# Spectral layers: one stored difference of sequence blocks fewer, formed anew in the second sweep

## The chip, the cores and the metric

The kernel runs on one core of one Trainium2 chip. The metric is the device time of one execution in microseconds (us); the kernel before is given as the median of its runs. The engines of the core are named as in the profile: PE (matmuls) and PEld (its weight loads), DVE (elementwise), ACT (copies, casts, activations), POOL (elementwise) and SP, which here issues the transfers between the chip's memory and the core's on-chip buffers in one queue, in order.

## The reference

Four layers follow each other on x of shape 2048 x 640 (sequence x features), each with a layer norm ahead of it and a residual add behind it: an attention over a dilated window, a spectral layer, and both again.

```python
def _B_ref(x, dft_seq_re, dft_seq_im, dft_hid_re, dft_hid_im):
    a = jnp.einsum("bsd,ed->bse", x, dft_hid_re)
    b = jnp.einsum("bsd,ed->bse", x, dft_hid_im)
    # Real((Cr + i*Ci) @ (a + i*b)) = Cr@a - Ci@b
    y = jnp.einsum("ts,bse->bte", dft_seq_re, a) - jnp.einsum("ts,bse->bte", dft_seq_im, b)
    return y

x = A_x
x = x + _A_ref(_layernorm(x, axis=-1), A_wqkv, A_wo)
x = x + _B_ref(_layernorm(x, axis=-1), B_dft_seq_re, B_dft_seq_im, B_dft_hid_re, B_dft_hid_im)
x = x + _A_ref(_layernorm(x, axis=-1), A_wqkv, A_wo)
x = x + _B_ref(_layernorm(x, axis=-1), B_dft_seq_re, B_dft_seq_im, B_dft_hid_re, B_dft_hid_im)
```

`_A_ref` is the window attention (32 heads of 20, 8 keys at distance 2); the change does not touch it. `_B_ref` is the spectral layer. All data are float32.

## The kernel before

The layers are numbered 0 to 3; 1 and 3 are the spectral ones (`LayerB`, with `self.li` 1 or 3). Such a layer multiplies first by the sequence matrices and then by the hidden ones. Each float32 operand is split into a rounded part (`hi`, cast by ACT, L1137) and its residual (`lo`, subtracted by DVE, L1138); a product then takes three passes of matmuls: hi times hi, hi times lo, lo times hi (`PASSES`, `product`, matmuls on L1148).

The sequence matrices arrive as `cs`, eight tiles of 256 outputs (real and imaginary part side by side) by 16 blocks of 128 rows. A raw block is 128 x 512 float32, 256 KB. Tiles 0 and 1 are worked with plain products (L1004). Tiles 2 to 7 are worked in three pairs (`pair(p)`, tiles t1 = 2p+2 and t2 = 2p+3) by a scheme of seven products in place of eight, as Strassen's in Winograd's form. For step i of eight, the four blocks are b11 = (t1, i), b21 = (t1, i+8), b12 = (t2, i) and b22 = (t2, i+8), and the scheme needs beside b11, b21, b22 these differences:

- x1 = b12 - b11 (the stored "t1")
- x3 = b22 - b12 (the stored "t3")
- x2 = b22 - x1
- x4 = b21 - x2

A pair has two sweeps over the eight steps. The first sweep takes the products with the plain blocks: aux (banks q), t (banks r) and m (banks w), and, for the features that the scheme leaves over, xt and pq (f1, f2) with all four blocks. The second sweep takes the products with x2 (banks q, "aux" in the profile), x3 (r, "t"), x4 (w, "m") and x1 (y, "xt" and "pq"). After it ACT and DVE combine the banks (L1301 to L1313) and store the result to `zb`.

In layer 1 only (`sums`), the first sweep also forms x1 and x3 on DVE (L1225, in place, in the buffers of b11 and b12) and stores both to the chip's memory, to `tb` (L1227). The second sweep, in both layers, loads x1 and x3 from `tb` (L1221) and b22 and b21 from `cs` (L1126), and forms x2 and x4 on DVE (L1225), each in place: x2 overwrites b22, x4 overwrites b21.

Raw blocks go through nine buffers in rotation (five "win", two "xa", two halves of "e2", L1204); split blocks (views) through eight in layer 1, ten in layer 3 (L1205). A buffer is loaded again when its readers are done, a store out of it included. PE's order is the program's order. The order of DVE, ACT and SP is made at build time by a scheduler with modelled times, so that work of later steps and pairs stands among that of earlier ones. In layer 1 the first sweeps also prepare the hidden weights on ACT and DVE (`b_prep`, L1161 to L1197); in the last pair's second sweep the operands of the hidden stage are prepared (`hid_load`, `prep`, L1328 and L1357), whose matmuls are on L1393.

## Time and profile before

| | |
|---|---|
| runs of the kernel before | 1699.35, 1698.45, 1706.01 us; median 1699.35 us |
| span of the profiled execution | 1700.9 us, 1.55 us above the median of the runs; no other time of that execution is listed |
| granted PE clock over the span | 1.000 |
| memory read and written | 319.75 MB and 119.67 MB, 258 GB/s over the span |
| layer 1, from the first product of the first pair to the hidden stage | 439.7 to 735.2 us |
| layer 3, the same | 1280.4 to 1574.2 us |

The page gives busy time and share of the span by engine; below it, chains and waits name what an engine stood waiting for. "DVE zo L1138" reads as the instruction of line 1138 on DVE that writes a buffer named zo. A row of the stretches gives the start and end, the length, then each engine's busy time with the number of its instructions. In the timeline a row starts with its start and its duration; idle time ahead of it stands in square brackets with what ended it. Instructions of one engine overlap a little in it: on DVE a following instruction of 0.68 us can start 0.60 us after the one ahead.

### The profile page before, as it was taken

The page shows a single profiled execution, that of the slowest core. Times are in us where ns is not written, and L with a number is a line of the kernel's source. Part 1 is how long each engine was busy: PE and PEld are TensorE (multiplying, and loading weights), DVE is VectorE, ACT ScalarE, POOL GpSimd, SP SyncE. Part 2 cuts the span into 40 slices and gives each one's busy share as a digit, 9 for nine tenths or more (in the row PEclk, how much of TensorE's full clock was granted, in tenths as well). Part 3 has the DMA queues.
Part 4 walks back from the last instruction along what each step waited for, and adds up shares of the span by engine and source line. Part 5 has one row for each costly group of instructions (what it writes and reads, how often), then busy time and mean ns, then how long its engine had stood idle before and what let it go on. Part 6 is the DMA issues. An engine that isn't in the chain of part 4 may idle for free.

```text
span 1700.9 us, 25512 instructions
## 1 busy us (share of the span) xinstructions
PE 1679.7 (99%) x8558; PEld 1464.6 (86%) x8558; DVE 1339.2 (79%) x2034; ACT 794.0 (47%) x1617; POOL 625.8 (37%) x588
## 2 busy tenths in 40 slices
PE   9999999989999999999999999999999999999999
PEld 7888988868888887899988889988888888888999
DVE  6999999978588786788639999999784656657784
ACT  5664644544354443536554335444444544444231
POOL 4899999950000000000028988999400000000000
PEclk9999999999999999999999999999999999999999
DMA  8996668857899989986377866788666776787942
GB/s 295 315 322 227 221 227 307 271 206 265 287 370 322 370 270 354 351 331 225 122 226 239 270 217 204 246 284 295 212 234 208 225 228 215 242 282 270 362 164 93
DMA packets 263139, 441.13 MB, mean 259 GB/s; under 512 B 21824, under 2 KB 126016, under 8 KB 260704
## 3 DMA queue, kind: packets, MB, share of 16 engines
q1 hardware_dynamic: 259808, 437.55, 75.7%
q10 hardware_dynamic: 3200, 1.97, 0.4%
q8 instruction: 67, 1.10, 0.3%
q14 instruction: 64, 0.52, 0.1%
HBM read 319.75 MB, written 119.67 MB: 258 GB/s over the span
## 4 chain that ended last, share of the span: by engine, by line
PE 76%; DVE 10%; POOL 6%; DMA 4%; issue 2%; ACT 0%; SPq 0%; DVEq 0%; POOLq 0%; ACTq 0%
PE m L381 19%; PE t L1148 7%; PE aux L1148 7%; PE m L1148 7%; PE pq L1148 5%; PE xt L1148 5%; PE m L1393 4%; PE aux L1393 4%; PE m L1004 3%; PE t L1004 3%; DVE pr L450 2%; PE aux L531 2%; DVE pr L490 2%; POOL pr L509 2%; PE xt L1393 2%
## 5 line engine op out<-in xcount | busy, mean ns | idle before, releaser
L381 PE MATMUL m<-r,s 128*128 128x480 f32 x1920 | 434.5, 381 | 0.6 <-ACT stg L388 0.4
L381 PEld LDWEIGHTS m<-r,s 128*128 128x128 f32 x1920 | 355.4, 188 | 53.5 <-ACT stg L388 0.8
L193 POOL TENSOR_TENSOR stats<-stats,mhalf 128x1 f32<-128x1 f32 (+1 forms) x40 | 29.2, 730 | 512.2 <-ACT stats L189 503.8
L509 POOL TENSOR_TENSOR pr<-pr 128x640 f32<-128x640 f32 x126 | 207.8, 1650 | 23.1 <-DVE pr L490 21.7
L450 DVE TENSOR_TENSOR pr<-pq,win 128x1280 f32<-128x1280 f32 x128 | 189.9, 1484 | 13.8 <-DMA win<-kvb 7.8
L490 DVE TENSOR_TENSOR pr<-pq,win 128x1280 f32<-128x1280 f32 x128 | 190.3, 1487 | 3.7 <-POOL zo L511 1.2
L453 POOL TENSOR_TENSOR pr<-pr 128x640 f32<-128x640 f32 x115 | 164.9, 1434 | 11.2 <-DVE pr L450 11.2
L460 DVE TENSOR_REDUCE lg<-pr 128x64 f32<-128x640 f32 (+1 forms) x128 | 112.7, 881 | 8.0 <-POOL pr L453 7.9
L510 POOL TENSOR_TENSOR pr<-pr 128x320 f32<-128x320 f32 x126 | 112.0, 889 | 9.9
L388 ACT COPY stg<-m 128x480 f32<-128x480 f32 x128 | 71.0, 555 | 92.9 <-PE m L381 69.1
L1004 PE MATMUL m<-s,r 128*128 128x512 f32 x366 | 111.2, 392 | 1.6 <-DMA s<-c0b 1.3
L1004 PE MATMUL t<-s,r 128*128 128x512 f32 x366 | 110.3, 390 | 0.0
L531 PE MATMUL aux<-r2a,ot 128*128 128x320 f32 x540 | 84.7, 310 | 0.7 <-ACT s L369 0.7
L531 PEld LDWEIGHTS aux<-r2a,ot 128*128 128x128 f32 x540 | 81.1, 188 | 2.8 <-ACT s L369 1.2
L1004 PEld LDWEIGHTS m<-s,r 128*128 128x128 f32 x366 | 67.6, 188 | 16.1 <-DMA s<-c0b 1.9
L1004 PEld LDWEIGHTS t<-s,r 128*128 128x128 f32 x366 | 68.7, 188 | 14.5
L1137 ACT CAST zo<-win 128x512 fp32r<-128x512 f32 x76 | 47.2, 621 | 65.4 <-PE xt L1148 30.0
L423 ACT COPY pq<-qs 128x320 f32<-128x320 f32 x64 | 27.5, 430 | 106.0 <-DVE pr L490 73.4
L1138 DVE TENSOR_TENSOR zo<-win,zo 128x512 fp32r<-128x512 f32 x76 | 52.1, 688 | 23.7 <-ACT zo L1137 23.3
L511 POOL TENSOR_TENSOR zo<-pr 128x160 f32<-128x160 f32 x126 | 67.1, 532 | 9.9
L1004 PE MATMUL xt<-s,r 128*128 128x512 f32 x183 | 68.6, 389 | 0.0
L468 ACT ACTIVATE lg<-lg 128x128 f32<-128x128 f32 x64 | 20.3, 317 | 74.6 <-DVE lg L479 74.4
(531 smaller groups left out, 3650.2 us busy)
## 6 DMA issues: line engine op xcount, KB each, us to landing
win<-cs_in SPq DMA_DIRECT2D x192, 256.0 KB, 3.8
win<-kvb SPq DMA_DIRECT2D x96, 440.0 KB, 5.3
win<-kvb SPq DMA_DIRECT2D x64, 360.0 KB, 5.0
kvb<-stg SPq DMA_DIRECT2D x60, 320.0 KB, 4.9
xa<-cs_in SPq DMA_DIRECT2D x66, 256.0 KB, 3.6
e<-cs_in SPq DMA_DIRECT2D x64, 256.0 KB, 3.9
r<-zb SPq DMA_DIRECT2D x12, 1280.0 KB, 5.9
win<-tb SPq DMA_DIRECT2D x56, 256.0 KB, 4.4
```

The source lines that it names most:

```text
L381: nc.tensor.matmul(mt[g][:, : 3 * F], st[:, a, k], wq[q][:, b, k], start=n == 0, stop=n == 14)
L388: nc.scalar.copy(sgs[q][:, :, j % 2], mt.pop(g)[:, : 3 * F].rearrange("p (a f) -> p a f", f=FE))
L450: nc.vector.tensor_tensor(pr, q, wview(u, jp, 0, [[1, FE]]), op=ALU.mult)
L453: nc.gpsimd.tensor_tensor(pv[:, :, 0:10], pv[:, :, 0:10], pv[:, :, 10:20], op=ALU.add)
L460: nc.vector.tensor_reduce(lgs[u][:, :, 2 * jp : 2 * jp + 2].rearrange("p h j w -> p (j w) h"), prq.pop((u, jp)), axis=AX.X, op=ALU.add,)
L490: nc.vector.tensor_tensor(pr.rearrange("p j w (h d) -> p j w h d", d=DH), lgs[u][:, :, 2 * jp : 2 * jp + 2].rearrange("p h j w -> p j w h" ...
L509: g.tensor_tensor(pr[:, :, 0:4], pr[:, :, 0:4], pr[:, :, 4:8], op=ALU.add)
L510: g.tensor_tensor(pr[:, :, 0:2], pr[:, :, 0:2], pr[:, :, 2:4], op=ALU.add)
L531: nc.tensor.matmul(m[:, :320], oT[(c, j)][:, a, k], wo_s["w"][:, b, k, e * 320 : (e + 1) * 320], start=(i, k) == (0, 0), stop=(i, k) == (2 ...
L1004: self.last = nc.tensor.matmul(self.z[t][k], self.xn[c][:, a, j, k * P : (k + 1) * P], self.ct[s][:, b], start=s == 0 and i == 0, stop=s = ...
L1148: nc.tensor.matmul(bank, w(a, kb), hl[b], start=start and (a, b) == (0, 0), stop=stop and (a, b) == (1, 0), skip_group_check=True,)
L1393: nc.tensor.matmul(bank[:, :320], s[:, a, k], w[:, b], start=start and (k, a, b) == (0, 0, 0), stop=stop and (k, a, b) == (KD - 1, 1, 0), ...
```

## The change

The difference x3 = b22 - b12 is no longer formed and stored in the first sweep of layer 1. In the second sweep, in both layers, b12 is loaded from `cs` in the place of x3 from `tb`, and DVE forms x3 in b12's buffer, ahead of x2 because x2 overwrites b22. `tb` keeps one difference per step, x1.

```diff
-    tb = [dr.tile([P, NP, 2, 512], F32, name=f"tb_{p}") for p in range(NPAIR)]
+    tb = [dr.tile([P, NP, 512], F32, name=f"tb_{p}") for p in range(NPAIR)]
...
-            def t_sum(n, i, o, a, b):
+            def t_sum(o, a, b):
                 v.tensor_tensor(o, a, b, op=ALU.subtract)
-                if n in names:
-                    nc.sync.dma_start(t_slot(n, i), o)
                 return o
...
                     if sums:
-                        t_sum("t1", i, b11, b12, b11)
-                        t_sum("t3", i, b12, b22, b12)
+                        nc.sync.dma_start(t_slot(i), t_sum(b11, b12, b11))
...
-                    x1, b22, x3, b21 = t_raw("t1", i), raw(t2, NP + i), t_raw("t3", i), raw(t1, NP + i)
+                    x1, b22, b12, b21 = t_raw(i), raw(t2, NP + i), raw(t2, i), raw(t1, NP + i)
                     s1, s2, s3 = (self.x_slot(m, i, XTAGS) if last and (m, i) in self.xlate else self.x_kept(m, i) for m in (1, 2, 3))
-                    x2 = t_sum("t2", i, b22, b22, x1)
+                    x3 = t_sum(b12, b22, b12)
+                    x2 = t_sum(b22, b22, x1)
                     self.product(q, s2, split(x2), False, i == NP - 1)
                     self.product(r, s3, split(x3), *ends)
-                    x4 = t_sum("t4", i, b21, b21, x2)
+                    x4 = t_sum(b21, b21, x2)
                     self.product(w, self.x_plain(*k2(i), 256), split(x4), *ends)
                     self.product(y, s1, split(x1), *ends)
```

In all, 24 subtractions and 24 stores of 256 KB leave layer 1's first sweeps; 48 subtractions enter the second sweeps; 48 loads of 256 KB read `cs` and no longer `tb`. The scheduler's order changes with it on DVE, ACT and SP, in the pairs and at the start of layer 1's hidden stage; PE's and POOL's orders are the same row for row. In the new file the subtraction is on L1223, the store on L1264, the load from `tb` on L1219, and the lines behind the pair stand four lower.

SP at the start of the third pair of layer 1, first sweep. Before (win_6517 is the buffer of a b12, xa_6567 that of a b11):

```order
L1227 DMA tb_146<-win_6517 128x512
L1126 DMA win_6633<-cs_in 128x512
L1027 DMA zb_5_133<-s_955_6042 512x1x128
L1126 DMA win_6688<-cs_in 128x512
L1227 DMA tb_146<-xa_6567 128x512
L1227 DMA tb_146<-win_6572 128x512
L1126 DMA e_724_4650<-cs_in 128x512
L1126 DMA win_6692<-cs_in 128x512
L1109 DMA zo_1067_6695<-xc_4_124 128x512
```

After:

```order
L1126 DMA win_6668<-cs_in 128x512
L1126 DMA e_724_4650<-cs_in 128x512
L1264 DMA tb_146<-xa_6547 128x512
L1126 DMA win_6725<-cs_in 128x512
L1126 DMA win_6729<-cs_in 128x512
L1264 DMA tb_146<-xa_6606 128x512
L1126 DMA e_724_4650<-cs_in 128x512
L1126 DMA win_6781<-cs_in 128x512
```

The stores out of the win buffers of b12 are gone; the loads into those buffers, which stood behind them, have no store to wait for.

DVE at the turn from the first to the second pair of layer 1: the adds that empty the banks (L1303 to L1311 before, L1299 to L1307 after), among splits and sums of the next pair. Before:

```order
L149 TENSOR_TENSOR pr_934_5916<-pr_906_5730,pr_934_5916 128x2x320
L1225 TENSOR_TENSOR win_5565<-e_724_4650,win_5565 128x512
L1303 TENSOR_TENSOR s_809_5153<-t_811_5163,s_808_5152 128x512
L1303 TENSOR_TENSOR s_809_5153<-t_812_5164,s_808_5152 128x512
L1138 TENSOR_TENSOR zo_895_5630<-xa_5621,zo_895_5630 128x512
L1138 TENSOR_TENSOR e_896_5639<-win_5623,e_896_5639 128x512
```

After (L147 and L149 are pieces of `b_prep`):

```order
L1305 TENSOR_TENSOR s_809_5137<-xt_5151,s_809_5137 128x512
L1307 TENSOR_TENSOR s_807_5135<-xt_5151,s_807_5135 128x512
L1138 TENSOR_TENSOR stg_5638<-e_724_4650,stg_5638 128x512
L147 SCALAR_TENSOR_TENSOR pr_953_6014<-pr_943_5954,pr_953_6014 128x2x32
L1138 TENSOR_TENSOR ot_5656<-win_5616,ot_5656 128x512
L1305 TENSOR_TENSOR s_809_5137<-pq_5152,s_809_5137 128x512
L1307 TENSOR_TENSOR s_807_5135<-pq_5152,s_807_5135 128x512
```

The next pair's x3 sum (L1225 on win_5565) no longer stands ahead of the adds, nor does the piece of L149; the piece of L147 now stands ahead of the last two.

DVE in the last step of the third pair's second sweep, layer 1. Before (L1225 on win_7310 is x2, on win_7314 x4; L1138 out of xa_7312, win_7310, win_7308 are the residuals of x3, x2, x1; L1366 prepares the hidden stage):

```order
L1225 TENSOR_TENSOR win_7310<-win_7310,win_7308 128x512
L1366 TENSOR_TENSOR r_2_1154_7205<-r_0_1153_7202,r_2_1154_7205 128x640 x2
L1138 TENSOR_TENSOR e_1177_7327<-xa_7312,e_1177_7327 128x512
L1138 TENSOR_TENSOR zo_1176_7318<-win_7310,zo_1176_7318 128x512
L1225 TENSOR_TENSOR win_7314<-win_7314,win_7310 128x512
L1138 TENSOR_TENSOR ot_7346<-win_7308,ot_7346 128x512
```

After (x3 on xa_7287, x2 on win_7285, x4 on win_7289):

```order
L1362 TENSOR_TENSOR r_2_1154_7178<-r_0_1153_7175,r_2_1154_7178 128x640 x2
L1223 TENSOR_TENSOR xa_7287<-win_7285,xa_7287 128x512
L1223 TENSOR_TENSOR win_7285<-win_7285,win_7283 128x512
L1138 TENSOR_TENSOR e_1177_7303<-xa_7287,e_1177_7303 128x512
L1223 TENSOR_TENSOR win_7289<-win_7289,win_7285 128x512
L1138 TENSOR_TENSOR ot_7322<-win_7283,ot_7322 128x512
L1138 TENSOR_TENSOR zo_1176_7294<-win_7285,zo_1176_7294 128x512
```

The residual of x2 (zo) now has x3, x4 and the residual of x1 (ot) ahead of it that stood behind it, or nowhere, before.

## The prediction

> **What bounds the kernel now.** I read the page's busy shares first, then the chain that ended last.

> ```profile
> span 1700.9 us, 25512 instructions
> PE 1679.7 (99%) x8558; PEld 1464.6 (86%) x8558; DVE 1339.2 (79%) x2034; ACT 794.0 (47%) x1617; POOL 625.8 (37%) x588
> ```

> PE leaves 1700.9 - 1679.7 = 21.2 us of the span unused, in both layer types together. The changed code runs only in the three pairs of each spectral layer, so I cut the trace into the twelve sweeps, first and second of each pair, layer 1 and then layer 3. Columns: stretch, length, busy time (and instructions) of PE, PEld, DVE, ACT, POOL, granted clock, DMA share, GB/s.

> ```profile
> 439.70:493.00 53.30, 53.30 (x235) 44.08 (x236) 37.84 (x62) 23.64 (x42) 0.00 (x0) 1.00 0.98 341
> 493.00:536.40 43.40, 43.40 (x194) 35.93 (x193) 37.89 (x62) 25.36 (x44) 0.00 (x0) 1.00 0.94 332
> 536.40:591.80 55.40, 55.04 (x242) 45.01 (x241) 43.30 (x72) 24.34 (x42) 0.00 (x0) 1.00 1.02 363
> 591.80:635.20 43.40, 43.40 (x194) 35.93 (x193) 35.23 (x57) 23.09 (x39) 0.00 (x0) 1.00 0.83 281
> 635.20:691.60 56.40, 55.06 (x242) 45.09 (x241) 35.25 (x56) 21.06 (x35) 0.00 (x0) 1.00 0.99 353
> 691.60:735.20 43.60, 43.60 (x195) 36.12 (x194) 38.00 (x59) 23.98 (x39) 0.00 (x0) 1.00 0.83 294
> 1280.40:1334.80 54.40, 54.40 (x240) 44.67 (x239) 28.18 (x43) 25.11 (x43) 0.00 (x0) 1.00 0.68 218
> 1334.80:1378.30 43.50, 43.50 (x194) 36.02 (x193) 29.16 (x46) 21.67 (x36) 0.00 (x0) 1.00 0.70 224
> 1378.30:1432.70 54.40, 54.40 (x242) 45.05 (x241) 30.16 (x47) 22.34 (x37) 0.00 (x0) 1.00 0.68 218
> 1432.70:1476.20 43.50, 43.50 (x194) 36.02 (x193) 29.66 (x47) 21.49 (x36) 0.00 (x0) 1.00 0.71 223
> 1476.20:1530.60 54.40, 54.40 (x242) 45.05 (x241) 30.45 (x47) 22.32 (x37) 0.00 (x0) 1.00 0.85 295
> 1530.60:1574.20 43.60, 43.60 (x195) 36.12 (x194) 33.20 (x51) 21.46 (x36) 0.00 (x0) 1.00 0.79 273
> ```

> In every second sweep PE is busy for the whole stretch, and in layer 3 in the first sweeps too. PE loses time in two places only, the starts of the second and third pair of layer 1: 55.40 - 55.04 + 56.40 - 55.06 = 1.70 us. The waits of PE name them (columns: who waited for whom, total us, times, longest), first at the third pair's start, then at the second's; the last row is PE's longest wait anywhere, outside these stretches.

> ```profile
> PE t L1148 <- ACT zo L1137: 1.1, 1, 1.1
> PE t L1148 <- DVE zo L1138: 0.2, 1, 0.2
> ```

> ```profile
> PE pq L1148 <- DVE s L1311: 0.2, 1, 0.2
> PE xt L1148 <- DVE s L1311: 0.2, 1, 0.2
> ```

> ```profile
> PE m L1004 <- ACT r L933: 2.1, 1, 2.1
> ```

> So the stages of the change are bound by PE, and the change adds or removes no matmul. Nothing but these 1.7 us can be won there. Lost can be as much as a second sweep comes to wait for DVE.

> **First sweep of layer 1: removed work.** Per step one subtraction on DVE and one 256 KB store on SP's queue go, 24 of each. The price of a subtraction, its duration as min/median/max:

> ```profile
> L1225 DVE TENSOR_TENSOR win<-win,win x33: 680/686/694, 447.9 to 1563.5; 128x512 f32<-128x512 f32 x33
> ```

> Per sweep that frees 8 x 0.686 = 5.5 us of DVE. DVE has room there and PE does not wait for it, so this alone is worth nothing, except where DVE is full: at the turn from the first pair to the second. There DVE's adds L1311, which empty two PSUM banks, come 0.2 + 0.2 = 0.4 us late. One removed subtraction (of 0.69 us) stood shortly ahead of them in DVE's queue, which would free them by more than they are late; but a step of the hidden weights (L147) now stands between them, and earlier ones of these steps have moved away. I take half, 0.2 us; bounds 0 and 0.4.

> The store matters through SP's in-order queue: a load into a raw buffer can't be issued before the store out of that buffer has landed. A wait of SP in layer 1, then the rows behind the 1.1 us stall (issues from the timeline, then the chain):

> ```profile
> SPq L1126 <- DMA tb<-win: 9.2, 10, 2.1
> ```

> ```profile
> 647.86 1.10 SPq L1227 DMA_DIRECT2D tb<-win  x1
> ...
> 651.73 0.33 SPq L1126 DMA_DIRECT2D win<-cs_in  x1
> ```

> ```profile
> 652.47 5.33 DMA tb<-xa
> 657.81 6.52 DMA xa<-cs_in
> 665.00 0.70 DVE zo L1138
> ```

> The store at 647.86 is of the difference that goes (its buffer held b12). The load at 651.73 into the same buffer waited for it, 651.73 - 647.86 = 3.9 us, and behind that load stood the store of xa (which stays), the load of xa, the split, and PE. Without the first store the row of issues moves up by as much as 3.9 us, against 1.1 + 0.2 = 1.3 us of stall. DMA share is 0.99 to 1.02 in these first sweeps, and 8 x 256 KB = 2.1 MB less per sweep is, at 353 GB/s, 5.9 us of transfer less. I take the whole 1.3 us. Bounds: 0, if the kept store of xa sets the end anyway, to 1.3 us.

> **Second sweeps: added work.** Per step a load from tb becomes a load of b12 from cs_in, of the same size:

> ```profile
> win<-cs_in SPq DMA_DIRECT2D x192, 256.0 KB, 3.8
> ...
> win<-tb SPq DMA_DIRECT2D x56, 256.0 KB, 4.4
> ```

> 3.8 against 4.4 us to landing, 48 times, with two steps of raw buffers ahead: nothing either way.

> DVE gets one subtraction more per step, x3, and x2 now stands behind it, because x2 overwrites b22, which x3 reads. Behind x2 wait its split and PE's first product of the step, and x4. Before, a step has 2 subtractions and 4 residuals of a split, 6 x 0.686 = 4.1 us; after, 7 x 0.686 = 4.8 us. PE needs four products of 1.36 us, 5.44 us (one chain row from each layer):

> ```profile
> 702.52 1.36 PE aux L1148 x6
> ...
> 1385.12 1.36 PE aux L1148 x6
> ```

> So DVE stays the faster one in the steady state. Per sweep it gets 8 x 0.686 = 5.5 us at most, 8 x 0.60 = 4.8 us where instructions follow each other (starts 0.60 apart, below). Its unused time per second sweep, from the first table, is 43.40 - 37.89 = 5.5, 43.40 - 35.23 = 8.2, 43.60 - 38.00 = 5.6 us in layer 1 and 14.3, 13.8, 10.4 us in layer 3. Layer 3 hides it: 0. In layer 1 it just fits, if the gaps come ahead of the work. The tightest is the third pair, whose end also holds the first operands of the next stage. Its tail, DVE and then PE:

> ```profile
> 725.50 0.68 DVE L1138 TENSOR_TENSOR zo<-win,zo 128x512 fp32r<-128x512 f32 x1
> 726.10 0.68 DVE L1225 TENSOR_TENSOR win<-win,win 128x512 f32<-128x512 f32 x1
> ...
> 729.56 1.52 PE L1148 MATMUL aux<-zo,pr 128*128 128x512 f32 x6
> ...
> 743.80 1.48 PE L1393 MATMUL m<-pr,zo 128*128 128x320 f32 x9
> ```

> DVE has no gap here, yet it is ahead of PE: the residual of x2 is ready at 725.50 + 0.68 = 726.2 and used at 729.56, a lead of 3.4 us. In the changed order the residual of x2 in this last step stands behind x3, x4 and another residual, three rows more, 1.8 us. That leaves 3.4 - 1.8 = 1.6 us for what earlier steps have not absorbed: 7 x 0.6 = 4.2 us against 5.6 us of gaps. I expect no wait, and allow 0 to 2.6 us here (4.2 - 1.6, nothing absorbed); I put 0.7 us, a quarter, into the sum. The other two layer-1 sweeps: 0, with DVE freed by 5.5 us in the first sweep on either side of them. The stage behind reads its third set of operands only at 743.80, so it has more lead than this.

> **Sum**: -1.3 - 0.2 + 0.7 = -0.8 us. The profiled execution (1700.9) stands 1.55 us above the median of the runs, 1699.35, so I take the sum from the median, 1699.35 - 0.8: 1698.5 us. What a measurement can tell from no change is 0.5%, 8.5 us; this is far inside.

> **Rivals.**

> 1. The stall moves instead of going (1699.4 us, chance 0.22). The kept store of xa and its 5.33 us of landing still set the load behind it, and x3 before x2 costs some tenths. For it: the chain runs through a store that stays. Against: that store was itself issued late, behind the load that waited 3.9 us.

> 2. DVE becomes the bound of layer 1's second sweeps (slower; chance 0.13). Place: x3 ahead of x2 in DVE's queue. It decides where DVE's gaps can't be used, because they are waits for a view that PE has still to free. Price: 5.5 us added less 3.4 us of lead is 2.1 us per sweep, three sweeps 6.3 us, 1705.7 us; with the removed stalls 1704. Only with half the lead as well used up, 3 x (5.5 - 1.7) = 11.4 us, 1710.8 us, does it leave the 8.5 us: chance 0.05. Against it: 4.8 us of DVE to 5.44 us of PE in a step. [...]

> 3. PE's busy time hides waiting, and lighter DMA shortens the matmuls (faster by over 8.5 us; chance 0.02). It would need 8.5 us of the 6 x 97.9 = 587 us that the six pairs take (97.9 = 54.40 + 43.50), 1.4%: 1690 us or less. Against: six matmuls take 1.36 us in layer 1 at a DMA share of 0.83 and in layer 3 at 0.70 alike. [...]

> **How the numbers follow.** The forecast (1697.4 to 1699.3) has 0.63, rival 1 0.22, rival 2 0.13, rival 3 0.02. Low end: all 1.7 us gone, 1697.65, and the runs' own scatter downward, 1699.35 - 1698.45 = 0.9, rounded down: 1696.5. High end: 1699.35 with the third pair's 2.6 us, 1702.0, and 0.9 of scatter: 1702.9; most of rival 2 stays outside. Faster by over 0.5%: rival 3 and a trace of luck, 0.03. Slower: the far end of rival 2, 0.05. Within: 0.92.

> **What would show it.** In the changed profile: PE's wait of 1.1 us on the split at the third pair's start gone, and the waits on the adds that empty xt and pq too; second sweeps of 43.4 to 43.6 us, all PE, with DVE 4 to 5.5 us fuller; the third first sweep near 55.1 us; stores to tb halved to 24; SP's waits for tb stores about halved. Wrong, if PE waits for DVE in second sweeps at the products of x2 (aux), if layer 3's stretches grow, or if a first sweep stalls longer than before.

## The result, and the profile after

The changed kernel takes 1728.5 us (median of 4 runs, 1727.8 to 1729.9) against 1702.5 us of the kernel before beside it; the ratio is 1.0154, 95% interval 1.0133 to 1.0176. It is slower by some 26 us. The prediction was 1698.5 us with 0.05 for slower.

The head of the page after; before it was a span of 1700.9 us, with PE busy 1679.7 us and DVE 1339.2 us.

```profile
span 1727.4 us, 25515 instructions
PE 1690.0 (98%) x8558; PEld 1467.2 (85%) x8558; DVE 1343.2 (78%) x2058; ACT 785.4 (45%) x1617; POOL 626.7 (36%) x588
```

Layer 1's six sweeps after, cut as in the prediction (columns as there):

```profile
437.90:491.30 53.40, 53.40 (x236) 43.82 (x235) 30.97 (x51) 21.76 (x40) 0.00 (x0) 1.00 0.88 289
491.30:540.10 48.80, 45.52 (x192) 36.70 (x192) 40.87 (x67) 22.79 (x41) 0.00 (x0) 0.97 0.90 296
540.10:602.20 62.10, 56.58 (x242) 45.99 (x242) 43.09 (x72) 27.02 (x50) 0.00 (x0) 0.97 0.94 319
602.20:646.60 44.40, 44.19 (x194) 35.81 (x193) 34.55 (x56) 19.32 (x35) 0.00 (x0) 1.00 0.74 230
646.60:707.50 60.90, 56.90 (x241) 45.85 (x240) 32.25 (x53) 21.24 (x35) 0.00 (x0) 0.97 0.86 296
707.50:758.30 50.80, 46.23 (x193) 37.04 (x192) 41.51 (x66) 23.98 (x41) 0.00 (x0) 0.97 0.80 268
```

They take 320.4 us where they took 295.5: 24.9 of the 26.5 us that the span grew are lost here. PE's idle time in them is 17.6 us (1.7 before), and PE is busy 302.8 us (293.8 before) with no matmul more: 15.9 us more are waiting, 9.0 us are slower matmuls, at a granted clock of 0.97 in four of the stretches. Layer 3's pairs are nearly as long as they were (306.6 us before, 308.3 after, from the first product of the pairs to the hidden stage). The transfer share fell in every stretch (0.74 to 0.94 here, 0.83 to 1.02 before), so a busier memory isn't what makes PE wait.

The five longest waits of PE in these stretches, 15.0 of the 17.6 us (who waited for whom, total us, times, longest):

```profile
PE aux L1148 <- ACT s L1297: 3.7, 1, 3.7
PE t L1148 <- DVE s L1272: 3.3, 1, 3.3
PE t L1148 <- ACT zo L1137: 3.2, 2, 2.7
PE aux L1148 <- ACT zo L1137: 2.5, 1, 2.5
PE pq L1148 <- DVE s L1307: 2.3, 2, 1.5
```

L1272 adds the banks t into c11 at the turn from first to second sweep, L1297 copies the banks aux at the end of a pair, and L1307 is the last add out of xt and pq there: in these three rows PE waits for banks to be emptied. The two rows on L1137 are casts (half of a split) in the third pair's sweeps. VectorE (DVE in the views) isn't full where that happens: it is busy for 40.87 of 48.80 us in the stretch of the first of these waits. Its rows at the first turn, in the timeline (start, duration, idle time ahead in brackets):

```profile
489.43 0.68 DVE L1138 TENSOR_TENSOR zo<-win,zo 128x512 fp32r<-128x512 f32 x1
492.45 0.69 DVE L1223 TENSOR_TENSOR win<-xa,win 128x512 f32<-128x512 f32 x1 [2.33 <-DMA xa<-cs_in]
...
495.46 0.69 DVE L1272 TENSOR_TENSOR s<-t,s 128x512 f32<-128x512 f32 x1
```

and PE's last product into these banks ahead of that add, and the one that waits for it:

```profile
485.69 1.52 PE L1148 MATMUL t<-e,r 128*128 128x512 f32 x6
...
496.20 2.93 PE L1148 MATMUL t<-zo,r 128*128 128x512 f32 x6 [3.27 <-DVE s L1272]
```

VectorE stands 2.3 us at a subtraction (L1223) whose raw block hasn't landed. Five rows behind it in the same queue stands the add that PE waits for, though PE had finished its bank at 485.69 + 1.52 = 487.2 us and ScalarE's copy, the add's other operand, ended at 491.2 us. From 430 to 750 us the waits of VectorE's sums (the subtractions that form x1 to x4) for a load are, before (L1225; the five rows sum to 4.7 us) and after (L1223; 34.1 us, all of it at sums of second sweeps and nearly all at x3, the first sum of a step):

```profile
DVE xa L1225 <- DMA win<-cs_in: 1.4, 1, 1.4
DVE xa L1225 <- DMA xa<-cs_in: 1.4, 2, 1.0
DVE e L1225 <- DMA win<-cs_in: 0.7, 1, 0.7
DVE win L1225 <- DMA e<-cs_in: 0.6, 1, 0.6
DVE win L1225 <- DMA win<-cs_in: 0.6, 1, 0.6
```

```profile
DVE win L1223 <- DMA xa<-cs_in: 11.3, 6, 3.5
DVE win L1223 <- DMA win<-cs_in: 10.7, 4, 6.1
DVE win L1223 <- DMA e<-cs_in: 5.1, 2, 4.0
DVE e L1223 <- DMA win<-cs_in: 4.6, 5, 2.5
DVE xa L1223 <- DMA win<-cs_in: 2.4, 2, 1.7
```

The loop closes through SP: a raw block is loaded when the split that frees its buffer is done, so a late VectorE makes later loads. The row of SP's waits for such a split in the same time, before and after (with a second row of after that is used further below):

```profile
SPq L1126 <- DVE zo L1138: 10.7, 18, 1.8
```

```profile
SPq L1126 <- DVE zo L1138: 26.4, 25, 4.2
...
SPq L1126 <- DMA tb<-win: 12.7, 9, 3.3
```

This row alone decides nothing: it is 16.8 us in a_orddve below, which loses no time.

### The profile page after: what moved, and what is told of

The parts are those of the page before. It is cut to its first block, busy times and chain, and to the rows that moved or that the text cites. A ratio compares the mean times of both kernels' runs of the same rounds, so it can differ in the third digit from the quotient of the medians.

```text
span 1727.4 us, 25515 instructions
## 1 busy us (share of the span) xinstructions
PE 1690.0 (98%) x8558; PEld 1467.2 (85%) x8558; DVE 1343.2 (78%) x2058; ACT 785.4 (45%) x1617; POOL 626.7 (36%) x588
## 4 chain that ended last, share of the span: by engine, by line
PE 52%; DVE 19%; DMA 16%; POOL 5%; issue 4%; ACT 2%; SPq 1%; DVEq 0%; ACTq 0%; POOLq 0%
PE m L381 15%; DVE pr L450 4%; PE aux L1389 4%; PE m L1389 4%; PE t L1148 4%; PE aux L1148 3%; DVE pr L490 3%; PE m L1148 3%; DMA win<-cs_in 3%; DMA wbd<-pr 3%; PE pq L1148 2%; PE xt L1148 2%; PE m L1004 2%; PE t L1004 2%; PE t L1389 2%
## 5 line engine op out<-in xcount | busy, mean ns | idle before, releaser
L450 DVE TENSOR_TENSOR pr<-pq,win 128x1280 f32<-128x1280 f32 x128 | 190.0, 1484 | 14.3 <-DMA win<-kvb 10.2
L1004 PE MATMUL m<-s,r 128*128 128x512 f32 x366 | 111.4, 392 | 1.1 <-DVE s L991 1.1
L1004 PE MATMUL t<-s,r 128*128 128x512 f32 x366 | 110.3, 390 | 0.0
L1137 ACT CAST zo<-win 128x512 fp32r<-128x512 f32 x76 | 47.0, 620 | 75.7 <-PE xt L1148 34.9
L1004 PEld LDWEIGHTS t<-s,r 128*128 128x128 f32 x366 | 68.7, 188 | 14.6
L1004 PEld LDWEIGHTS m<-s,r 128*128 128x128 f32 x366 | 67.3, 188 | 16.1 <-DVE s L991 2.7
L1004 PE MATMUL xt<-s,r 128*128 128x512 f32 x183 | 68.7, 390 | 0.0
L1148 PE MATMUL t<-zo,r 128*128 128x512 f32 x204 | 55.9, 409 | 7.3 <-DVE s L1272 3.3
L1138 DVE TENSOR_TENSOR zo<-win,zo 128x512 fp32r<-128x512 f32 x76 | 51.8, 688 | 12.4 <-ACT zo L1137 12.2
## 6 DMA issues: line engine op xcount, KB each, us to landing
win<-cs_in SPq DMA_DIRECT2D x220, 256.0 KB, 4.0
xa<-cs_in SPq DMA_DIRECT2D x76, 256.0 KB, 3.9
e<-cs_in SPq DMA_DIRECT2D x74, 256.0 KB, 4.2
```

The costliest lines, as they stand in the source:

```text
L450: nc.vector.tensor_tensor(pr, q, wview(u, jp, 0, [[1, FE]]), op=ALU.mult)
L1004: self.last = nc.tensor.matmul(self.z[t][k], self.xn[c][:, a, j, k * P : (k + 1) * P], self.ct[s][:, b], start=s == 0 and i == 0, stop=s = ...
L1148: nc.tensor.matmul(bank, w(a, kb), hl[b], start=start and (a, b) == (0, 0), stop=stop and (a, b) == (1, 0), skip_group_check=True,)
```

## The experiments

All runs below the first two rows were timed beside the kernel before (medians 1702.6 to 1703.4 us). "Pairs" is the time from the first product of layer 1's pairs to the first matmul of its hidden stage (the first such products stand among those of the plain tiles, at 425.7 us before and 423.9 after; the 439.7 and 437.9 us at which the stretches begin are where the plain tiles end); "sums ahead" counts, in VectorE's order, the sums of the coming second sweep that stand ahead of the first bank addition (c11) at the three turns; "sums wait" is the time that VectorE's sums waited for loads in the pairs. The runs are in the order in which they were made.

| run | what it is | median us | ratio (95%) | pairs us | sums ahead | sums wait us |
|---|---|---|---|---|---|---|
| before | | 1703 | 1 | 309.3 | 2, 2, 2 (of 16) | 4.7 |
| the change | first measurement | 1728.5 | 1.0154 (1.0133 to 1.0176) | 334.4 | 5, 6, 5 (of 24) | 34.1 |
| add_only | addition alone | 1703.9 | 1.0005 (0.9995 to 1.0014) | 308.1 | 3, 3, 3 | 13.0 |
| rem_only | removal alone | 1718.9 | 1.0098 (1.0081 to 1.0116) | 326.1 | 4, 4, 4 (of 16) | 30.0 |
| keep_sub | store alone removed | 1722.6 | 1.0113 (1.0096 to 1.0130) | 327.6 | 5, 5, 6 | 27.4 |
| l3_only | change in layer 3 alone | 1704.9 | 1.0011 (1.0001 to 1.0021) | 310.4 | 2, 2, 2 (of 16) | 4.5 |
| after_again | the change | 1731.0 | 1.0164 (1.0149 to 1.0179) | 334.3 | 5, 6, 5 | 36.1 |
| a_noprep | no weight preparation | 1749.6 | 1.0279 (1.0253 to 1.0306) | 325.0 | 6, 6, 5 | 55.0 |
| a_pin | preparation held back | 1721.5 | 1.0110 (1.0088 to 1.0132) | 329.1 | 4, 6, 3 | 34.9 |
| a_store | a dummy store put back | 1709.3 | 1.0040 (1.0025 to 1.0055) | 316.4 | 3, 2, 3 | 12.1 |
| a_ordadd | good order, three queues | 1702.4 | 0.9997 (0.9987 to 1.0007) | 307.5 | 3, 3, 3 | 12.0 |
| a_ordsp | good order, SP | 1717.3 | 1.0094 (1.0061 to 1.0126) | 321.8 | 4, 5, 4 | 19.6 |
| a_orddve | good order, VectorE and ScalarE | 1703.3 | 1.0005 (0.9992 to 1.0018) | 307.0 | 3, 3, 3 | 8.6 |
| a_ordslow | order for a slower memory | 1720.3 | 1.0104 (1.0079 to 1.0128) | 322.2 | 3, 1, 3 | 5.2 |
| a_mixprep | good order, early preparation | 1709.4 | 1.0034 (1.0022 to 1.0046) | 316.4 | 3, 3, 3 | 11.8 |
| a_mixrest | changed order, good preparation | 1729.4 | 1.0151 (1.0133 to 1.0169) | 334.6 | 5, 6, 5 | 52.2 |
| a_ordd | good order, VectorE | 1715.4 | 1.0069 (1.0052 to 1.0087) | 315.8 | 3, 3, 3 | 10.6 |
| a_orda | good order, ScalarE | 1718.3 | 1.0090 (1.0070 to 1.0110) | 323.3 | 5, 6, 6 | 36.9 |
| a_sumlate | changed order, good sums | 1717.2 | 1.0092 (1.0070 to 1.0114) | 318.0 | 3, 3, 3 | 5.8 |
| a_sumearly | good order, changed sums | 1729.2 | 1.0166 (1.0144 to 1.0188) | 330.8 | 5, 6, 3 | 42.6 |

### Addition or removal

My first theory after the result (A) came from the waits of ScalarE and VectorE in the changed trace: the preparation of the hidden weights (`b_prep`, a chain of loads, casts and stores in two single buffers) stands earlier in their queues. Its rivals were the added subtraction (B) and the other source of the load (C). "Split n" counts the residuals (L1138) of layer 1's pairs that stand ahead in VectorE's order.

The first kernel is the one before, with only the second sweeps changed:

```diff
-                    x1, b22, x3, b21 = t_raw("t1", i), raw(t2, NP + i), t_raw("t3", i), raw(t1, NP + i)
+                    x1, b22, x3, b21 = t_raw("t1", i), raw(t2, NP + i), raw(t2, i), raw(t1, NP + i)
...
+                    x3 = t_sum("", i, x3, b22, x3)
```

> The first sweeps stay as before (x3 is subtracted and stored there), and only the second sweeps of layers 1 and 3 form x3 anew from b12 and b22; nobody reads the stored x3. Theory A (the removed store and subtraction let the build-time scheduler pull the preparation of the hidden weights forward in VectorE's and ScalarE's queues, and that blocks the emptying of the PSUM banks at the turns): here the preparation's rounds stand in VectorE's order almost where they stood before (first piece of each of the five rounds ahead of split 7, 26, 52, 74, 100, against 7, 26, 52, 72, 96 before and 7, 24, 43, 67, 84 after), so the time is that of before, 1697 to 1704 us, and layer 1's pairs take 295 to 298 us. Theory B (the added subtraction in front of x2 makes VectorE late, the second rival of the prediction): the addition is all here, so 1720 to 1730 us and layer 1's pairs near 320 us. Theory C (x3's raw block now comes by a load of another tensor that is late): as B, 1715 to 1730 us.

The addition costs next to nothing, +0.8 us (-0.9 to +2.4), though VectorE is fuller than in any other kernel here (busy 244 of 308 us in the pairs). B and C fall. Its fullest stretch, and PE in it:

```profile
480.00:520.00 40.00, 40.00 (x178) 33.12 (x177) 37.91 (x62) 22.64 (x40) 0.00 (x0) 1.00 1.00 356
```

The removal alone:

```diff
-                    x1, b22, b12, b21 = t_raw(i), raw(t2, NP + i), raw(t2, i), raw(t1, NP + i)
+                    x1, b22, x3, b21 = t_raw(i), raw(t2, NP + i), t_raw(i), raw(t1, NP + i)
...
-                    x3 = t_sum(b12, b22, b12)
```

> The first sweeps as in the change (x3 neither subtracted nor stored), and the second sweeps load x1's slot a second time in x3's place, with no subtraction added: the products that should use x3 use x1, so this part of the result is another one, with the same number of loads, splits and products as before. Theory A: the preparation's rounds stand at split 7, 24, 41, 62, 83 of VectorE's order, pulled forward as after the change, so it is slow, 1712 to 1732 us, with the long waits of TensorE at the turns of layer 1. Theory B: nothing is added, so 1696 to 1702 us. Theory C: as B, 1696 to 1702 us.

```diff
                         nc.sync.dma_start(t_slot(i), t_sum(b11, b12, b11))
+                        t_sum(b12, b22, b12)
```

> The change, with x3 also subtracted in layer 1's first sweep as before but not stored: the store alone is removed there, and VectorE has one subtraction per step more than in the change. Theory A, with the store as the trigger: rounds at split 7, 24, 44, 68, 88, still ahead of before's, so slow, 1712 to 1730 us. Theory A, with the subtraction as the trigger: 1698 to 1705 us. Theory B: VectorE has more work than after the change, so at least 1728 us.

```diff
-                    x1, b22, x3, b21 = t_raw("t1", i), raw(t2, NP + i), t_raw("t3", i), raw(t1, NP + i)
+                    x1, b22 = t_raw("t1", i), raw(t2, NP + i)
+                    x3 = t_raw("t3", i) if sums else raw(t2, i)
+                    b21 = raw(t1, NP + i)
...
+                    if not sums:
+                        x3 = t_sum("", i, x3, b22, x3)
```

> Layer 1 as before (x3 stored and loaded), layer 3 alone forms x3 anew from the raw block. Theory A: the preparation's order is the one of before, and layer 3's pairs prepare no weights, so 1697 to 1704 us. Theory B, if it holds in both layers: half of the loss, 1709 to 1716 us, with layer 3's pairs longer by 10 us or more. Theory C: as B in layer 3.

Taking work away costs 16 us (rem_only), taking the store alone away costs 19 us with VectorE's work kept (keep_sub, which differs from add_only in the stores alone), and layer 3 has some 2 us of it (0.2 to 3.6). So most of the loss follows the removal, and of the removed work the store. Theory A had said so too, so these runs don't yet test its mechanism.

### Is it the weights' preparation?

> The changed kernel once more, beside the ones below on the same chip: 1724 to 1732 us by every theory.

```diff
         def b_prep(self, k):
...
+            for vs in ((0,), (1, 6), (5, 2), (4, 3)):
+                for x in vs:
+                    self.late.append(lambda x=x: nc.sync.dma_start(wbd[:, x * KD + k].rearrange("p e f -> p (e f)"), wre[:, k, :]))
+                yield
```

(all else that `b_prep` did is taken out)

> The change, with the preparation of the hidden weights taken out of ScalarE and VectorE: each piece only copies a block of the raw weights from DRAM to the place where the prepared one is stored, so the hidden layers use other weights and that part of the result is another one; the products are as many as before. Theory A (the preparation's chain, pulled forward, blocks VectorE and ScalarE at the turns): without the chain the loss goes, 1695 to 1702 us, and layer 1's pairs take 294 to 298 us. Theory D (what blocks is something else that the scheduler reordered, the sums of the second sweeps or the raw loads; the chain only stood near it): most of the loss stays, 1715 to 1730 us.

```diff
-                    if self.bprep and (p == 0 or i > 1):
+                    if self.bprep and i % 2 == 0:
                         next(self.bprep, None)
...
+                    if self.bprep and not last and i % 2 == 0:
+                        next(self.bprep, None)
...
-            nc.scalar.copy(y[:, 0, 0], wr[:, 0])
+            tc.keep_in_program_order(nc.scalar.copy(y[:, 0, 0], wr[:, 0]))
```

(the last edit at the first ScalarE and VectorE instruction of each piece)

> The change, with the same preparation put out every other step, one round of four pieces per sweep, and the first ScalarE and VectorE instruction of every piece kept behind the one written before it, so that the scheduler can't pull it forward: rounds start at split 7, 36, 68, 100, 132 of VectorE's order and end at 20, 54, 84, 120, 147, none across the emptying of banks. Theory A: 1695 to 1702 us. Theory D: 1715 to 1730 us, as the sums and the loads stay free to move.

```diff
-    tb = [dr.tile([P, NP, 512], F32, name=f"tb_{p}") for p in range(NPAIR)]
+    tb = [dr.tile([P, NP, 2, 512], F32, name=f"tb_{p}") for p in range(NPAIR)]
...
                         nc.sync.dma_start(t_slot(i), t_sum(b11, b12, b11))
+                        nc.sync.dma_start(tb[p][:, i, 1].rearrange("p (r t) -> p r t", r=2), b12)
```

> The change, with the second store of a step put back with plain b12 in it, which nobody reads; the subtraction stays in the second sweep. Theory A, with the store as the trigger: rounds at split 7, 24, 50, 72, 96, close to those of before (7, 26, 52, 72, 96), so 1697 to 1706 us. Theory B (the added subtraction): 1725 us or more, since the store adds traffic and takes nothing away.

Theory A fails twice. Without the preparation the pairs still take 325.0 us, 15.7 more than before (another 29 us of that run, by which it is slower than any expectation, lie ahead of the pairs, whose first product comes at 454.9 us instead of 425.7; most are two waits of PE of 11.5 and 14.7 us in the first 70 us of the program, far from the change, and why they are there stays open). With the preparation held back they take 329.1. But a_store, which does strictly more than the change (24 stores that nobody reads), is 22 us faster than it, though still slower than theory A expected. That less work takes longer points at the order made at build time, which the next runs test.

### The order itself

From here on the instructions of single queues were forced, within layer 1's pairs, into an order taken from another build; "the good order" is that of add_only, without its first-sweep subtractions and stores of x3. The scheduler orders the queues that aren't forced anew, so SP's order differs from run to run where it is free (in a_orddve it is neither the changed kernel's nor that of a_ordadd). `ORDER` holds the instructions' numbers, one list for each engine that is forced; lines stand 7 to 9 lower in these kernels:

```diff
+    byname = {i.name: i for i in nc.cur_bb.bb.instructions}
+    for seq in ORDER:
+        for a, b in zip(seq, seq[1:]):
+            dep = mybir.DependencyInfo(mybir.DependencyClass.NoSync, mybir.DependencyReason.DATA)
+            tc.add_manual_dep(byname[f"I-{b}"], f"I-{a}", dep, reason="order")
```

> The change, instruction for instruction, with one thing forced by a table: in layer 1's pairs the instructions of VectorE, ScalarE and SP stand in the order that they have in the kernel which keeps the first sweep's subtraction and store of x3 and runs like before (that order, with those two left out). Theory E (the build's scheduler, with 24 stores less in its model, orders the three queues more tightly, and that order is what costs): 1697 to 1703 us, layer 1's pairs 306 to 311 us from their first product to the hidden layer's first (before 309.3, changed 334.4), and no wait of TensorE over 1.5 us in them. Theory F (the loss lies in the work as it runs, whatever the order: other loads, buffers freed at other times): 1720 us or more.

> As the run with all three queues forced, but only VectorE's and ScalarE's orders are forced; SP is left to the scheduler. Theory E, if VectorE's and ScalarE's order carries it: 1697 to 1706 us; if SP's does: 1712 us or more. Theory F: 1720 us or more.

> As the run with all three queues forced, but only SP's order (loads and stores) is forced; VectorE and ScalarE are left to the scheduler, which puts the preparation's rounds at split 7, 24, 50, 73, 97. Theory E, if SP's order carries it: 1697 to 1706 us; if VectorE's and ScalarE's does: 1712 us or more, unless the scheduler brings them near to before's order by itself. Theory F: 1720 us or more.

> As the run with all three queues forced, with the order of a program that had three stores more per step of layer 1 than the change (two in the first sweep, one in the second), and without these stores: an order made for a slower memory. Theory E: 1696 to 1706 us, at most 1 to 2 us below before, since the waits of TensorE in before's pairs sum to 1.7 us. Theory F: 1720 us or more.

This settles the main question. The changed program in the order of add_only runs like the kernel before, 0.9997 (0.9987 to 1.0007), and forcing VectorE's and ScalarE's order is enough, with SP's made anew to go with it. In a_orddve PE doesn't wait once in the pairs; the stretch with the first turn:

```profile
480.00:520.00 40.00, 40.00 (x178) 33.15 (x177) 35.09 (x57) 21.60 (x37) 0.00 (x0) 1.00 0.95 329
```

SP's order alone gives back less than half. And the order isn't simply "too tight": the one made with three stores more per step (a_ordslow) is slow too, against theory E's expectation, though its sums wait for loads for only 5.2 us. PE's longest wait there, 4.1 us at 608.3 us, stands behind a cast that ScalarE held for 4.9 us until PE had freed its view: again an in-order queue stands, but not for a load.

### What in the order

The two orders of VectorE around the first turn, without the preparation's pieces (A first sweep, B second sweep, then the step; S the sums x3, x2, x4 of a second sweep or x1 of a first, r the residual of a split; c11 the bank additions):

```
good     A6.S1 A7.r11 A7.r21 A7.S1 A7.r22 A7.r12 B0.S3 B0.S2 B0.S4 B0.r2 B0.r3 B0.r4 B0.r1 c11 c11 B1.S3 B1.S2 B1.S4 B1.r3
changed  B0.S3 B0.S2 B0.S4 A7.r11 A7.r21 A7.S1 A7.r22 A7.r12 B0.r2 B1.S3 B0.r3 B0.r4 B1.S2 B0.r1 c11 B1.S4 c11 B2.S3 B1.r2
```

In the changed order step 0's sums stand ahead of the last four splits of the first sweep, and two to three sums of the next step stand ahead of the additions that empty the banks. On average over layer 1 a sum of a second sweep has moved forward by 1.6 splits. Two pairs of runs take the parts apart: the preparation against the rest, then the sums against the rest.

> The change with VectorE's and ScalarE's orders forced in layer 1's pairs: sums, splits and the emptying of the banks in the good order (that of the kernel which keeps the store), the preparation of the hidden weights as early as the changed kernel has it (rounds at split 7, 24, 43, 67, 84). SP is left to the scheduler. If the preparation's early place costs: 1715 us or more, with waits of TensorE at the turns. If the order of sums and splits costs: 1699 to 1706 us.

> The reverse: sums, splits and the emptying of the banks in the changed kernel's order, the preparation at the places of the good one (rounds at split 7, 26, 52, 74, 100). If the preparation's early place costs: 1699 to 1706 us. If the order of sums and splits costs: 1715 us or more.

> The change with VectorE's order alone forced to the good one; ScalarE and SP are left to the scheduler, and the preparation's rounds come out at the good places. If VectorE's queue carries the loss: 1699 to 1706 us. If ScalarE's does: 1712 us or more.

> The change with ScalarE's order alone forced to the good one; VectorE and SP are left to the scheduler, and the preparation's rounds come out at the good places too (26, 52, 74, 100). If the preparation's place carries the loss, or ScalarE's queue: 1699 to 1706 us. If the order of sums and splits on VectorE carries it: 1712 us or more.

> The change with VectorE's and ScalarE's orders forced in layer 1's pairs to what the scheduler gave the changed kernel, but every sum on VectorE moved back to where it stands in the good order, after as many splits and bank additions as there (three of the next sweep's sums ahead of the first bank addition of a turn, not five or six). If the early sums cost: 1699 to 1711 us (the upper end, since the preparation keeps its early place, which cost 6 us alone). If the order of the splits costs: 1718 us or more.

> The reverse: the good order of VectorE and ScalarE with only the sums moved forward to where the changed kernel has them. If the early sums cost: 1715 us or more, with waits of TensorE for the bank additions at the turns. If the order of the splits costs: 1699 to 1706 us.

The early preparation costs 6 us by itself (1.0034, between the two ranges expected), and with it put back the whole loss stays (1.0151). The early sums alone, in orders of VectorE and ScalarE that are otherwise the good ones, cost some 27 us (1.0166), as much as the change. In a_sumearly VectorE at the first turn (sums on L1231, c11 on L1280), and PE behind it:

```profile
486.85 0.68 DVE L1146 TENSOR_TENSOR zo<-win,zo 128x512 fp32r<-128x512 f32 x1
494.47 0.69 DVE L1231 TENSOR_TENSOR win<-xa,win 128x512 f32<-128x512 f32 x1 [6.93 <-DMA win<-cs_in]
...
498.42 0.69 DVE L1280 TENSOR_TENSOR s<-t,s 128x512 f32<-128x512 f32 x1
```

```profile
499.15 3.25 PE L1156 MATMUL t<-zo,r 128*128 128x512 f32 x6 [5.72 <-DVE s L1280]
```

and the same two instructions in a_orddve, where the addition stands first and the sum waits for nothing:

```profile
490.19 0.69 DVE L1280 TENSOR_TENSOR s<-t,s 128x512 f32<-128x512 f32 x1
...
491.79 0.68 DVE L1231 TENSOR_TENSOR win<-xa,win 128x512 f32<-128x512 f32 x1
```

So early sums are enough for the loss. They aren't all that can be wrong with an order: with the sums put back alone (a_sumlate) 16 us of loss remain, just short of the range that would have blamed the splits. By the spans 8.7 us of them lie in layer 1's pairs, 3.2 in the hidden stage behind them and 2.8 in layer 3's pairs. The early preparation can account for about 6 of the 16 by a_mixprep; the rest goes with the order of the splits, or with both together. VectorE's or ScalarE's order alone (a_ordd, a_orda) gives back 14 and 11 us of the 26; each of the two runs fell into the range that blamed the other engine, so neither queue carries the loss alone. The parts don't add up, and which pairs of instructions make the remaining 16 us in a_sumlate stays open, as does most of the loss of a_ordslow. That each order is a fit of all queues to each other would explain it, but no run shows it.

## Why the prediction was wrong

**The chain of causes, as far as shown.** The removed stores change the model from which the build's scheduler orders the queues (a store put back for nothing brings 22 us back). It then puts the second sweeps' sums one to two splits earlier on VectorE (a_sumearly: enough for the loss). On the chip their raw blocks land later than that place needs (34.1 us of waits); VectorE's in-order queue stands, and the additions and splits behind it come late for PE. Late splits free raw buffers late, so the next loads are late as well; this last step is read from SP's waits (26.4 us for such splits, 10.7 before) and no run isolates it. Early sums aren't the only thing that the new order has wrong, as a_sumlate shows.

**First sweep, removed work.** "So this alone is worth nothing" is the step that failed. It priced the removed instruction and the removed store in the order of before, and for the order it had one term of at most 0.4 us at one turn (L1311, and L147 standing between). It saw that rows had moved, but took a moved row for a row's duration. The term that was missing is what a moved row that waits for a load holds up. rem_only measured the removal alone at +16 us, keep_sub that of the store alone at +19 us.

**The stall in the third pair, and the adds at the turn.** The prediction put the 1.1 us stall at the third pair's start; at 665.03 us it stands 29.8 us into the pair's first sweep, in its fifth step. In the good order the 1.7 us of waits before are gone (0.3 us left in a_ordadd, none in a_orddve), as the sum had it with -1.3 and -0.2. The reason given is shown only in part: add_only, which keeps the subtraction and the store, has no wait at the adds and 0.65 us at the stall, so about half of the stall and all of the rest went with the order; a_ordadd, that order without the two, has nothing of either. The 0.3 us in a_ordadd is the tail that the sum priced at +0.7; in the changed kernel the same tail waits 3.5 us (2.55 and 0.99 at the last product on aux), above the 2.6 allowed. a_ordadd measures the work alone at -0.5 us (-2.2 to +1.2); the sum said -0.8, and this interval can't tell it from nothing. In the changed kernel itself the stall grew to 2.7 us (the longest of the waits on ACT zo L1137 into t).

**Loads from `cs_in` in place of `tb`: "with two steps of raw buffers ahead: nothing either way".** True in the good order. In the changed one the lead was spent by the order: VectorE's 34.1 us of waits are for the raw blocks that the second sweeps load from `cs_in`.

**Second sweeps, added work.** Right in the good order. add_only has all of it, fills VectorE to 37.9 of 40 us, and costs 0.8 us (-0.9 to +2.4). So rival 2, on whose side the result fell, had the wrong reason (x3's work ahead of x2) and the wrong price (up to 1710.8 us). The waits do stand at x3, but rem_only, which forms no x3, waits 30.0 us at its other sums. Layer 3 was put at 0; l3_only measured +1.9 us (0.2 to 3.6).

**The clock.** The prediction's sum has no term for a lower clock, and the 2.1 us per sweep of its rival 2 are priced at their length alone. The changed kernel has waits of up to 3.7 us. Behind the wait of 3.27 us six matmuls took 2.93 us, where six of the same kind took 1.52 before it; of the 9.0 us that PE is busier in the pairs, the four stretches at 0.97 account for about 0.03 x 222.6 = 6.7 us, an estimate. A wait as short as those 2.1 us had such a price too: in a_sumlate two groups of matmuls ran slow behind one of 2.09 us (last section).

**The markers.** The stores to `tb` were halved as said, 14 + 5 + 5 = 24 (issues by line, with their durations and first and last start):

```profile
L1264 SPq DMA_DIRECT2D tb<-win x14: 326/379/1389, 423.7 to 687.9; - x14
...
L1264 SPq DMA_DIRECT2D tb<-e x5: 319/382/942, 451.8 to 698.4; - x5
L1264 SPq DMA_DIRECT2D tb<-xa x5: 320/327/438, 485.7 to 666.6; - x5
```

SP's waits for them were not halved: 12.7 us from 430 to 750 us for stores out of win, where before had 7.3 in the same time (9.2 over the whole run, the prediction's row). VectorE's second sweeps were 3.0 us fuller, 0.7 emptier and 3.5 fuller, not 4 to 5.5 fuller. The second sweeps (48.8, 44.4 and 50.8 us, against 43.4 to 43.6 forecast), the third first sweep (60.9 against 55.1) and PE's waits at the products on aux all went against the forecast, in layer 1 alone.

## What to carry to other kernels

Where a scheduler with modelled times orders in-order queues, taking work away is a change of the whole order, and its price is in no row of the old trace: read in the new order which instructions that wait for a load now stand ahead of those that empty a bank or free a buffer, and price what queues behind them. When a change that saves work comes out slower, build the new program in the old order before looking for a cause in the work; here that one run (a_ordadd) separated the two. An early instruction on an engine with much idle time isn't free: idle time in an in-order queue is of use only if it doesn't stand ahead of something that others need (here VectorE, busy 40.87 of 48.80 us, stood 2.33 us at one sum, and PE waited 3.27 us for the add behind it).

## What the runs showed of the hardware

PE's matmuls ran slow after some waits and not after others. After the wait of 3.27 us above six of them took 2.93 us, where six of the same kind had taken 1.52. In a_sumlate two groups ran slow after a wait of 2.09 us:

```profile
549.75 0.92 PE L1156 MATMUL pq<-e,r 128*128 128x512 f32 x3 [2.09 <-DVE s L1315]
...
551.18 2.73 PE L1156 MATMUL aux<-zo,r 128*128 128x512 f32 x6
553.71 1.98 PE L1156 MATMUL t<-e,r 128*128 128x512 f32 x6
```

and in a_sumearly one after three waits of 0.93, 0.84 and 0.92 us close to each other:

```profile
547.25 0.96 PE L1156 MATMUL m<-e,xr 128*128 128x512 f32 x3 [0.93 <-DVE s L1310]
549.05 0.97 PE L1156 MATMUL m<-e,xr 128*128 128x512 f32 x3 [0.84 <-DVE s L1310]
550.94 2.90 PE L1156 MATMUL xt<-zo,r 128*128 128x512 f32 x6 [0.92 <-DVE s L1315]
```

while a wait of 1.95 us in a_ordsp was followed by no such slowing:

```profile
496.08 1.66 PE L1155 MATMUL t<-zo,r 128*128 128x512 f32 x6 [1.95 <-DVE s L1279]
```

So in these traces the length of the longest wait doesn't tell which groups ran slow. The granted clock does show what goes with it. In the changed kernel's trace it falls from 1.00 to 0.50 four times in layer 1's pairs, at 495.7, 543.5, 680.0 and 751.7 us, for 3.41 us each time, and these starts lie 14, 40 and 21 times 3.41 us apart. In the 3.41 us ahead of each PE had idled 2.76, 3.34, 2.72 and 2.63 us. Of the stretches of 3.41 us counted from these starts, over the pairs, the one with the most idle time and no fall behind it has 1.50 us (from 550.30 us). Cut into stretches of this length, counted from their own falls, the three other traces read (stretch, length, PE busy, granted clock, DMA share, GB/s; a_sumlate, a_sumearly, a_ordsp):

```profile
547.80:551.21 3.41, 1.46 (x7) 1.00 1.03 309
551.21:554.62 3.41, 3.41 (x10) 0.50 1.02 347
```

```profile
547.50:550.91 3.41, 1.68 (x6) 1.00 0.99 316
550.91:554.32 3.41, 3.38 (x8) 0.50 0.93 301
```

```profile
491.27:494.68 3.41, 2.86 (x13) 1.00 0.60 197
494.68:498.09 3.41, 2.01 (x9) 1.00 0.90 295
```
